# Sparse attention with a mixture layer on one core: K of two batches kept on chip for the first sparse pairs

## The chip, the cores and the metric

One core of one Trainium2 chip runs the whole program. The time is microseconds on the device, the median of several runs; lower is better. The engines of the core are TensorE (PE, with PEld for its weight loads), VectorE (DVE), ScalarE (ACT), GpSimd (POOL) and SyncE (SP); DMA transfers are issued from the queues of SP, ACT and POOL.

## The reference

Block-sparse attention over 4 batches, 8 heads, 768 positions and head dimension 64, followed by one feed-forward layer; all inputs are float32. A query block of 32 sees the first and last block, its neighbours, itself, and three sampled blocks (the first and last query block see everything):

```python
scores = scale * np.matmul(q, k.transpose(0, 1, 3, 2))
mask = np.abs(blk_i - blk_j) <= 1
mask = mask | (blk_i == 0) | (blk_j == 0) | (blk_i == n_blocks - 1) | (blk_j == n_blocks - 1)
for qb in range(n_blocks):
    for kb in sampled_blocks[qb]:
        mask[qb * 32:(qb + 1) * 32, kb * 32:(kb + 1) * 32] = True
attn = softmax(np.where(mask, scores, -1e9))      # then @ v
x = attn_out.transpose(0, 2, 1, 3).reshape(3072, 512)
h = x @ w_in                                      # 512 x 2048
g = h * (1.0 / (1.0 + np.exp(-1.702 * h)))
return g @ w_out                                  # 2048 x 512
```

The weights arrive as 64-bit floats and are taken apart on the chip.

## The kernel before

The 3072 rows of x are 48 units of 64 rows, and 8 units are a chunk of 512 rows. The first four units are the dense ones, one per batch: the first and the last query block against all 24 key blocks. Each has four items (two pairs of head pairs, two halves of the keys). The other 44 are sparse: a pair of query blocks u of two batches (0 and 1, or 2 and 3) shares one K entry and one V entry, and each batch is one unit and one item. A sparse K entry has 12 slots of 32 keys for two batches: slots 0 to 2 and 9 to 11 are the sampled blocks of the two query blocks, 3 to 5 and 8 their neighbourhood, 6 and 7 the first and the last block.

K, Q and V entries live in rings of two buffers (`RING`; `kg`, `qt`, `vown`, `vmid`). `loads` (L227) issues the load of an entry when, in the order of the program, the last use of the entry two before it has been issued. `load_k` (L180) loads Q of the entry and K: four transfers for a dense unit; for a sparse pair the neighbourhood (L195, L196), the first and last block where the buffer doesn't hold them yet (L198), and six sampled slots with an address from a register (L205), three of them from the POOL queue while `early` is set. `load_v` (L207) loads V; for sparse pairs the sampled and neighbouring rows come by two gathers on the POOL queue (L223), the rest by SP (L219, L221).

The program has two stages. `first` (L713), the opening, runs the items of the first nine units, 16 dense and 5 sparse ones (items 0 to 20), with `early` set. For each item n it issues the scores of n on PE (L284 dense, L272 sparse), the running minimum on DVE (L295), the transposes of item n-1 (L323, copied out on ACT at L327), the exponentials of n on ACT (L302), what ACT has to do for the weights (the list `late`), the values of n-1 (L356 dense, L348 sparse), and then `loads`. Between them `weights` (L425) is stepped, at fixed items: it fetches the 64-bit words of a weight tile (`raw`, L447, three buffers, asked for two tiles ahead, from the ACT queue), turns them into float32 (`a`, three buffers; L456 on ACT, L490, L496, L500 on DVE), splits the result in two float32r parts (L503 on ACT, L464 on DVE), and for the second weight saves it (`ws`, L471) for later chunks. Each engine executes in the order in which the program issues to it.

Then come 96 ticks of `tick` (L673): six chunks of 16 tiles f of the inner dimension, each with the up product (L538 to L540), the gate and the down product (L585 to L590); the items of the next chunk are laid between them by `plan`. In the first 16 ticks the remaining weight tiles are converted; `win` keeps the 16 tiles of w_in, 4 KB per partition each.

Of the kernel before, what the change touches and what calls it, by code (L numbers as in the profile page):

```python
# [9 lines left out]
F32 = mybir.dt.float32  # L10
F32R = mybir.dt.float32r
# [7 lines left out]
P = 128  # L19
# [14 lines left out]
NN = CT // P  # L34
RING = 2
WRING = 3
LAG = 1
QT = 4
BIG = float(2 ** 33)
# [4 lines left out]
class Kernel:  # L44
# [4 lines left out]
    def __init__(self, ctx, tc, q, qd, kb, kT, v, vd, sb, w_in, w_out, out):  # L49
        self.tc, self.nc = tc, tc.nc  # L50
        self.q, self.qd, self.kb, self.kT, self.v, self.vd, self.sb = q, qd, kb, kT, v, vd, sb
        self.w64, self.out = (w_in.bitcast(I32), w_out.bitcast(I32)), out
        pool = lambda name, bufs, **k: ctx.enter_context(tc.tile_pool(name=name, bufs=bufs, **k))
        self.const = pool("const", 1)
        self.work = pool("work", 2)
        self.small = pool("small", 6)
        psum = pool("psum", 1, space=PSUM)
        dram = pool("dram", 1, space=DRAM)
        self.ws = [dram.tile([P, DM], F32, name=f"ws{f}") for f in range(NF)]
        self.bank = [psum.tile([P, 512], F32, name=f"bank{i}") for i in range(8)]  # L60
        c = self.const


        self.kg = [c.tile([P, 12, 2, NPAIR * BLK], F32, name=f"kg{i}") for i in range(RING)]
        self.qt = [c.tile([P, 2, NPAIR * UT], F32, name=f"qt{i}") for i in range(RING)]
        self.vown = [c.tile([P, 2, 2 * DM], F32, name=f"vown{i}") for i in range(RING)]
        self.vmid = [c.tile([P, 2 * DM], F32, name=f"vmid{i}") for i in range(RING)]
        self.win = [c.tile([P, 2 * DM], F32R, name=f"win{f}") for f in range(NF)]
        self.wout = [c.tile([P, 2 * DM], F32R, name=f"wout{i}") for i in range(WRING)]
        self.x = [(c.tile([P, NCT, CT], F32R, name=f"xhi{i}"), c.tile([P, NCT, CT], F32R, name=f"xlo{i}"))  # L70
                  for i in range(2)]
        self.kmidof, self.vmidof = [None] * RING, [None] * RING
        self.units, self.kent, self.vent, self.items = [], [], [], []

        def entry(of, **more):
            of.append({"n": len(of), "scores": 0, "values": 0, **more})
            return of[-1]

        def item(k, v, **more):
            k["scores"] += 1  # L80
            v["values"] += 1
            self.items.append({"n": len(self.items), "unit": self.units[-1], "k": k, "v": v, **more})

        for b in range(B):
            entry(self.units, b=b, u=None)
            k = entry(self.kent, b=b, u=None)
            for i in range(2):
                v = entry(self.vent, b=b, u=None, i=i)
                for half in range(2):
                    item(k, v, i=i, half=half, first=i + half == 0, end=i + half == 2)  # L90
        for b0 in range(0, B, 2):
            for u in range(NU):
                k, v = (entry(of, b=b0, u=u) for of in (self.kent, self.vent))
                for b in (b0, b0 + 1):
                    entry(self.units, b=b, u=u)
                    item(k, v, first=True, end=True)
        self.knext = self.vnext = 0
        self.early = True


# [76 lines left out]

    def load_k(self, e):  # L180
        nc, b, u = self.nc, e["b"], e["u"]
        r = e["n"] % RING
        kg = self.kg[r].rearrange("p n b c -> p n (b c)")
        if u is None:
            nc.sync.dma_start(out=self.qt[r][:, 0], in_=self.qd[:, b])
            kg, kT = (ap.rearrange("p (a s) -> p a s", a=NPAIR) for ap in (self.kg[r].rearrange("p n b c -> p (n b c)"), self.kT[b]))
            for i in range(2):
                for half in range(2):
                    at = slice(2 * i, 2 * i + 2), slice(S // 2 * half, S // 2 * (half + 1))
                    nc.sync.dma_start(out=kg[:, at[0], at[1]], in_=kT[:, at[0], at[1]])  # L190
            self.kmidof[r] = None
            return
        q0, kb = 2 * u + 1, self.kb[:, b // 2]
        nc.sync.dma_start(out=self.qt[r].rearrange("p b c -> p (b c)"), in_=self.q[:, b // 2, u])
        nc.sync.dma_start(out=kg[:, 3:6].rearrange("p n c -> p (n c)"), in_=kb[:, q0 - 1:q0 + 2].rearrange("p n c -> p (n c)"))  # L195
        nc.sync.dma_start(out=kg[:, 8], in_=kb[:, q0 + 2])  # L196
        if self.kmidof[r] != b:
            nc.sync.dma_start(out=kg[:, 6:8], in_=kb[:, 0:NB:NB - 1])  # L198
            self.kmidof[r] = b
        for j in range(2):  # L200

            queue = nc.gpsimd if self.early and j == 1 else nc.sync
            for i in range(NR):
                at = queue.value_load(self.sbr[0:1, q0 + j, i, 0:1], min_val=0, max_val=NB - 1)
                queue.dma_start(out=kg[:, 9 * j + i], in_=kb[:, bass.ds(at, 1)].rearrange("p o c -> p (o c)"))  # L205

    def load_v(self, e):  # L207
        nc, b, u = self.nc, e["b"], e["u"]
# [17 lines left out]

    def loads(self):  # L227

        more = True
        if not self.knext:  # L230
            self.load_k(self.kent[0])
            for e in self.vent[:RING]:
                self.load_v(e)
            self.knext, self.vnext = 1, RING
        while more:
            more = False
            if self.knext < len(self.kent) and (self.knext < RING or not self.kent[self.knext - RING]["scores"]):
                self.load_k(self.kent[self.knext])
                self.knext += 1
                more = True  # L240
            if self.vnext < len(self.vent) and (self.vnext < RING or not self.vent[self.vnext - RING]["values"]):
                self.load_v(self.vent[self.vnext])
                self.vnext += 1
                more = True
# [11 lines left out]
    def scores(self, g):  # L256
# [7 lines left out]
        if sparse:  # L264
            bi, n = un["b"] % 2, 2 * P
            kg = self.kg[r][:, :, bi].rearrange("p n (a s) -> p n a s", a=NPAIR)
            for i in range(2):
                for a in range(2):
                    for j in range(2):
                        for h in range(2):  # L270
                            pair, rows, c = 2 * i + a, slice(D * h, D * (h + 1)), 2 * a + j
                            nc.tensor.matmul(  # L272
                                sps[h][BLK * c:BLK * (c + 1), n * i:n * (i + 1)].rearrange("p (n s) -> p n s", s=BLK),
                                self.qt[r][rows, bi, UT * pair + BLK * j:UT * pair + BLK * (j + 1)],
                                kg[rows, 4 * j:4 * j + 8, pair], start=True, stop=True, tile_position=(D * h, BLK * c))
            parts = [(i, 0) for i in range(2)]
            bias = self.bias[:, un["u"]].rearrange("p (n o) -> p n o", o=1).broadcast_to([P, 8, BLK])
        else:
            kt = self.kg[r].rearrange("p n b c -> p (n b c)").rearrange("p (a s) -> p a s", a=NPAIR)
            i, half, n = g["i"], g["half"], S // 2  # L280
            for a in range(2):
                for h in range(2):
                    pair, rows = 2 * i + a, slice(D * h, D * (h + 1))
                    nc.tensor.matmul(sps[h][UT * a:UT * (a + 1), 0:n], self.qt[r][rows, 0, UT * pair:UT * (pair + 1)],  # L284
                                     kt[rows, pair, n * half:n * (half + 1)], start=True, stop=True, tile_position=(D * h, UT * a))
            parts = [(i, half)]
            bias = self.zero.broadcast_to([P, n])
# [137 lines left out]
    def weights(self):  # L425
# [11 lines left out]
        def scalar(f):  # L437
            if self.early:
                self.late.append(f)
            else:  # L440
                f()

        def fetch(k):
            def go():
                f, i = todo[k]
                raw = self.work.tile([P, 2 * DM], I32, name="raw", bufs=3)
                nc.scalar.dma_start(out=raw, in_=self.w64[i][f])  # L447
                tiles[k] = {"raw": raw.rearrange("p (a b) -> p a b", b=2)}

            if k < len(todo):  # L450
                scalar(go)

        def first(k):
            def go():
# [29 lines left out]
        for k, (f, i) in enumerate(todo):  # L484
# [2 lines left out]
            fetch(k + 2)  # L487
            raw, a = tiles[k]["raw"], tiles[k]["a"]
            low, high = raw[:, :, 0], raw[:, :, 1]
            nc.vector.tensor_scalar(out=a, in0=a, scalar1=3, scalar2=None, op0=ALU.logical_shift_left)  # L490
            yield
            rested = not self.early
# [320 lines left out]
```

## Time and profile before

| | |
|---|---|
| time, median of 3 runs | 773.05 us (771.04 to 773.26) |
| profiled execution, time | 774.74 us |
| profiled execution, span | 773.1 us |
| PE busy | 734.6 us (95%) |
| DVE busy | 412.9 us (53%) |
| ACT busy | 385.0 us (50%) |
| POOL busy | 53.2 us (7%) |
| bytes moved by DMA | 128.22 MB, 166 GB/s over the span |

The busy shares are means over the whole span; the stages differ, so the rows further down are taken stage by stage. Times in a trace count from the first instruction of the span. A row of the timeline gives start, length, engine, source line, operation, output and input, and in brackets how long the engine stood idle before it and what ended that.

### The profile page before, as it was taken

To read this page: it belongs to the slowest core of one execution; us is meant where nothing else is said; L and a number is where in the kernel's file an instruction comes from. 1 tells how busy PE (TensorE), PEld (TensorE's weight loads), DVE (VectorE), ACT (ScalarE), POOL (GpSimd) and SP (SyncE) were. 2 spreads that over 40 slices of the span, in tenths; PEclk is the share of its full clock that TensorE was granted. 3 is DMA by queue.
4 is the path that set the end of the run, shared out by engine and by line. 5 is a ranking of instruction groups with operands and counts; after the bars stand their busy time and mean duration, and the time that the engine had idled before them with its cause. 6 is when DMAs were issued, how large, how long until landed. Compare 5 with 4: busy or idle time off the path is not lost.

```text
span 773.1 us, 19315 instructions
## 1 busy us (share of the span) xinstructions
PE 734.6 (95%) x7584; PEld 571.4 (74%) x7584; DVE 412.9 (53%) x1076; ACT 385.0 (50%) x950; POOL 53.2 (7%) x79
## 2 busy tenths in 40 slices
PE   4986599999999999999999999999999999999997
PEld 2554477777777877877877877877877877888885
DVE  2885478998854454454454454454464454343333
ACT  3885466766645445445445445445444444333232
POOL 1022210110100000000000000000000000000000
PEclk9999899999999999999999999999999999999999
DMA  8999888788656435566444455434465410141111
GB/s 292 336 340 318 263 259 273 241 249 288 204 144 190 133 119 166 155 167 189 138 121 146 146 171 164 131 123 155 133 164 173 129 43 29 42 110 41 55 42 54
DMA packets 65469, 128.22 MB, mean 166 GB/s; under 512 B 7761, under 2 KB 31570, under 8 KB 65378
## 3 DMA queue, kind: packets, MB, share of 16 engines
q1 hardware_dynamic: 51202, 80.76, 34.6%
q0 software_dynamic: 6944, 24.72, 10.2%
q10 hardware_dynamic: 7232, 21.50, 8.4%
q8 instruction: 60, 0.98, 0.5%
q14 instruction: 31, 0.25, 0.1%
HBM read 116.47 MB, written 10.49 MB: 164 GB/s over the span
## 4 chain that ended last, share of the span: by engine, by line
PE 77%; DMA 9%; DVE 6%; ACT 4%; issue 2%; SPq 1%; ACTq 0%; DVEq 0%
PE bank L538 11%; PE bank L540 10%; PE bank L590 10%; PE bank L589 10%; PE bank L585 10%; PE bank L539 10%; PE bank L272 5%; PE bank L348 5%; PE bank L323 4%; DMA kg<-in_kb_dram 3%; DMA vown<-in_vd_dram 2%; DMA raw<-in_moe_w_in_dram 1%; ACT ex L302 1%; PE bank L356 1%; PE bank L411 1%
## 5 line engine op out<-in xcount | busy, mean ns | idle before, releaser
L538 PE MATMUL bank<-xhi,win 128*128 128x512 f32 x384 | 158.3, 412 | 1.6 <-DVE g L553 1.2
L553 DVE SCALAR_TENSOR_TENSOR g<-g,bank 128x512 f32<-128x512 f32 x83 | 57.1, 688 | 186.9 <-ACT g L546 186.9
L590 PE MATMUL bank<-wout,ghi 128*128 128x512 f32 x384 | 152.0, 396 | 0.0
L589 PE MATMUL bank<-wout,ghi 128*128 128x512 f32 x384 | 151.9, 396 | 0.0
L540 PE MATMUL bank<-xhi,win 128*128 128x512 f32 x384 | 151.1, 393 | 0.0
L539 PE MATMUL bank<-xlo,win 128*128 128x512 f32 x384 | 149.9, 390 | 0.0
L302 ACT ACTIVATE ex<-bank,nm 128x256 f32<-128x256 f32 (+1 forms) x208 | 99.8, 492 | 98.5 <-DVE nm L295 98.3
L546 ACT ACTIVATE g<-bank 128x512 f32<-128x512 f32 x96 | 57.6, 600 | 148.6 <-PE bank L540 148.6
L585 PE MATMUL bank<-wout,glo 128*128 128x512 f32 x384 | 107.7, 394 | 0.0
L527 DVE TENSOR_TENSOR wout<-wst,wout 128x512 fp32r<-128x512 f32 x80 | 55.5, 693 | 91.5 <-ACT wout L526 91.2
L558 ACT CAST ghi<-g 128x512 fp32r<-128x512 f32 x96 | 59.6, 620 | 70.8 <-DVE g L553 70.8
L538 PEld LDWEIGHTS bank<-xhi,win 128*128 128x128 f32 x384 | 72.1, 188 | 19.5 <-ACT wst L551 1.8
L585 PEld LDWEIGHTS bank<-wout,glo 128*128 128x128 f32 x384 | 72.5, 189 | 17.3
L590 PEld LDWEIGHTS bank<-wout,ghi 128*128 128x128 f32 x384 | 72.5, 189 | 16.8
L589 PEld LDWEIGHTS bank<-wout,ghi 128*128 128x128 f32 x384 | 72.1, 188 | 16.6
L540 PEld LDWEIGHTS bank<-xhi,win 128*128 128x128 f32 x384 | 72.1, 188 | 16.3
L327 ACT COPY pt<-bank 128x512 f32<-128x512 f32 (+1 forms) x120 | 61.3, 561 | 42.9 <-PE bank L323 42.4
L295 DVE CUSTOM_DVE_ANT_1 bank<-bank,bias 128x256 f32<-128x256 f32 x176 | 73.9, 440 | 15.2 <-PE bank L272 12.2
L539 PEld LDWEIGHTS bank<-xlo,win 128*128 128x128 f32 x384 | 72.3, 188 | 13.0
L223 POOL DMA_INDIRECT vown<-in_v_dram,vidx x44 | 43.2, 982 | 512.8 <-PE bank L348 490.9
L323 PEld LDWEIGHTS bank<-ident,ex 128*128 128x128 f32 x448 | 52.3, 144 | 21.5 <-ACT ex L302 9.0
L566 DVE TENSOR_TENSOR glo<-g,ghi 128x512 fp32r<-128x512 f32 x96 | 65.7, 685 | 0.7 <-ACT ghi L558 0.7
(75 smaller groups left out, 788.8 us busy)
## 6 DMA issues: line engine op xcount, KB each, us to landing
wst<-ws SPq DMA_DIRECT2D x80, 256.0 KB, 2.8
kg<-in_kb_dram SPq DMA_DIRECT2D x142, 128.0 KB, 3.0
kg<-in_kb_dram SPq DMA_DIRECT2D x22, 384.0 KB, 5.4
raw<-in_moe_w_in_dram ACTq DMA_DIRECT2D x16, 512.0 KB, 6.7
raw<-in_moe_w_out_dram ACTq DMA_DIRECT2D x16, 512.0 KB, 4.4
kg<-in_kT_dram SPq DMA_DIRECT2D x16, 384.0 KB
vown<-in_vd_dram SPq DMA_DIRECT2D x8, 768.0 KB, 5.9
qt<-in_q_dram SPq DMA_DIRECT2D x22, 256.0 KB
```

The costliest lines, as they stand in the source:

```text
L295: nc.vector.tensor_tensor_reduce(out=at, in0=at, in1=bias, scale=-SCALE, scalar=3.0e38, op0=ALU.add, op1=ALU.min, accum_out=un["nm"][:, ha ...
L302: nc.scalar.activation(out=ex, in_=sps[h][:, n * k:n * (k + 1)], func=AF.Exp, bias=un["nm"][:, half, c:c + 1], scale=-1.0, accum_out=un["r ...
L323: nc.tensor.transpose(ps[:, m], g["ex"][h, i][:, k * P:(k + 1) * P], self.ident)
L327: copies.append(lambda pt=pt, ps=ps, m=m: nc.scalar.copy(out=pt[:, 0:m], in_=ps[:, 0:m]))
L538: nc.tensor.matmul(h, wih[:, k], hi[:, k], start=(k == 0), stop=False)
L539: nc.tensor.matmul(h, wih[:, k], lo[:, k], start=False, stop=False)
L540: nc.tensor.matmul(h, wil[:, k], hi[:, k], start=False, stop=(k == NCT - 1))
L558: self.nc.scalar.copy(out=ghi, in_=self.g[m][0])
L566: self.nc.vector.tensor_tensor(out=glo, in0=g, in1=ghi.bitcast(F32), op=ALU.subtract)
L585: nc.tensor.matmul(o[n], glo[:, tk[n]], woh, start=False, stop=last)
L589: nc.tensor.matmul(o[n], ghi[:, tk[n]], woh, start=(f == 0), stop=False)
L590: nc.tensor.matmul(o[n], ghi[:, tk[n]], wol, start=False, stop=False)
```

## The change

The dense units are taken in the order of batches 2, 3, 0, 1. K of the dense units of batches 0 and 1 goes into a buffer of its own, `kres`, instead of the ring. While `early` is set, K of a sparse pair is copied from `kres` to the slots of `kg` by GpSimd, one copy per slot (128 partitions x 256 float32), 12 or 10 per pair; for the six sampled slots the block's number is loaded into a register first. These copies are issued to GpSimd's queue where `loads` reaches the entry: entries 4 and 5 need not wait for the two dense entries before them, which no longer use the ring. The load of Q is a step of its own. A fourth buffer for weight words, `raw4`, is used by every fourth tile while `early` is set, and words are asked for three tiles ahead there. `kres` and `raw4` take the place of the tiles 9 to 15 of `win` (28 KB per partition), which are allocated when the conversion comes to tile 9.

```diff
+NWIN = 9
-        self.win = [c.tile([P, 2 * DM], F32R, name=f"win{f}") for f in range(NF)]
+        self.win = [c.tile([P, 2 * DM], F32R, name=f"win{f}") for f in range(NWIN)]
...
+        self.opening = ExitStack()
+        early = self.opening.enter_context(tc.tile_pool(name="opening", bufs=1))
+        self.kres = early.tile([P, 2, NPAIR, S], F32, name="kres")
+        self.raw4 = early.tile([P, 2 * DM], I32, name="raw4")
...
-        for b in range(B):
+        for b in (2, 3, 0, 1):
             entry(self.units, b=b, u=None)
...
+    def load_q(self, e):
+        b, u, qt = e["b"], e["u"], self.qt[e["n"] % RING]
+        if u is None:
+            self.nc.sync.dma_start(out=qt[:, 0], in_=self.qd[:, b])
+        else:
+            self.nc.sync.dma_start(out=qt.rearrange("p b c -> p (b c)"), in_=self.q[:, b // 2, u])
...
         if u is None:
-            nc.sync.dma_start(out=self.qt[r][:, 0], in_=self.qd[:, b])
+            k = e["kt"] = self.kres[:, b] if b < 2 else self.kg[r].rearrange("p n b c -> p n (b c)").rearrange("p (a s) -> p a s", a=NPAIR)
...
-                    nc.sync.dma_start(out=kg[:, at[0], at[1]], in_=kT[:, at[0], at[1]])
-            self.kmidof[r] = None
+                    nc.sync.dma_start(out=k[:, at[0], at[1]], in_=kT[:, at[0], at[1]])
+            if b >= 2:
+                self.kmidof[r] = None
             return
-        q0, kb = 2 * u + 1, self.kb[:, b // 2]
-        nc.sync.dma_start(out=self.qt[r].rearrange("p b c -> p (b c)"), in_=self.q[:, b // 2, u])
+        q0, middle = 2 * u + 1, self.kmidof[r] != b
+        self.kmidof[r] = b
+        if self.early:
+            kg = self.kg[r].rearrange("p n b (a s) -> p n b a s", s=BLK)
+            src = self.kres.rearrange("p b a (n s) -> p n b a s", s=BLK)
+            for n, at in [(3, q0 - 1), (4, q0), (5, q0 + 1), (8, q0 + 2)] + [(6, 0), (7, NB - 1)] * middle:
+                nc.gpsimd.tensor_copy(out=kg[:, n], in_=src[:, at])
+            for j in range(2):
+                for i in range(NR):
+                    at = nc.gpsimd.value_load(self.sbr[0:1, q0 + j, i, 0:1], min_val=0, max_val=NB - 1)
+                    nc.gpsimd.tensor_copy(out=kg[:, 9 * j + i], in_=src[:, bass.ds(at, 1)].rearrange("p o b a s -> p (o b) a s"))
+            return
...
-            queue = nc.gpsimd if self.early and j == 1 else nc.sync
...
     def loads(self):
+        k = self.kent
+        passed = lambda n: n < RING or not k[n - RING]["scores"]
+
+        def kfree(n):
+            e = k[n]
+            last = e["n"] - (4 if e["u"] is not None and e["n"] < 6 else RING)
+            return n < RING or not k[last]["scores"]
...
+            if self.qnext < len(k) and passed(self.qnext):
+                self.load_q(k[self.qnext])
+                self.qnext += 1
+                more = True
+            if self.knext < self.qnext + self.early and self.knext < len(k) and kfree(self.knext):
+                self.load_k(k[self.knext])
...
+        asked = [0]
+
         def fetch(k):
-            def go():
+            def go(k, own):
                 f, i = todo[k]
-                raw = self.work.tile([P, 2 * DM], I32, name="raw", bufs=3)
+                raw = self.raw4 if own else self.work.tile([P, 2 * DM], I32, name="raw", bufs=3)
...
+            for n in range(asked[0], min(k + 1 + self.early, len(todo))):
+                scalar(lambda n=n, own=self.early and n % 4 == 3: go(n, own))
+                asked[0] += 1
...
+            if i == 0 and f == NWIN:
+                self.opening.close()
+                late = self.pool("late", 1)
+                self.win += [late.tile([P, 2 * DM], F32R, name=f"win{n}") for n in range(NWIN, NF)]
```

## Rows read from the trace of the kernel before

**Rows 1.** Busy time by stretch: from:to, length, each engine busy, granted PE clock, DMA share, GB/s.
```profile
8.00:58.00 50.00, 43.36 (x581) 27.47 (x583) 38.78 (x144) 37.56 (x110) 4.88 (x7) 1.00 0.99 352
58.00:98.50 40.50, 25.21 (x604) 17.54 (x599) 20.90 (x79) 19.49 (x63) 10.49 (x14) 0.87 0.93 288
98.50:215.00 116.50, 113.31 (x1127) 87.67 (x1124) 98.37 (x228) 79.61 (x184) 8.34 (x8) 1.00 0.77 247
```
**Rows 2.** Timeline of PE, end of the dense part and sparse items 16 to 19.
```profile
57.38 0.92 PE L356 MATMUL bank<-vown,pt 128*64 128x64 f32 x24 [1.18 <-DMA vown<-in_vd_dram]
58.23 1.09 PE L272 MATMUL bank<-kg,qt 64*32 64x256 f32 x32
...
65.01 1.37 PE L356 MATMUL bank<-vown,pt 128*64 128x64 f32 x24 [4.89 <-ACT pt L327]
66.31 1.96 PE L272 MATMUL bank<-kg,qt 64*32 64x256 f32 x32
...
69.80 0.30 PE L348 MATMUL bank<-vown,pt 128*32 128x64 f32 x2
...
72.61 1.32 PE L272 MATMUL bank<-kg,qt 64*32 64x256 f32 x32 [1.45 <-DMA vmid<-in_v_dram]
...
78.02 1.09 PE L272 MATMUL bank<-kg,qt 64*32 64x256 f32 x32
```
**Rows 3.** Timeline of PE, the last sparse item and the first up matmul.
```profile
89.06 2.34 PE L272 MATMUL bank<-kg,qt 64*32 64x256 f32 x32 [7.26 <-DMA kg<-in_kb_dram]
...
98.48 0.50 PE L538 MATMUL bank<-xhi,win 128*128 128x512 f32 x1
```
**Rows 4.** Timeline of ACT and its queue, 54 to 64 us.
```profile
54.53 0.34 ACTq L471 DMA_DIRECT2D ws<-a  x1
...
63.93 0.66 ACT L456 ACTIVATE a<-raw 128x512 f32<-128x512 f32 x1 [5.88 <-DMA ws<-a]
```
**Rows 5.** Timeline of SP's queue, the last dense V load.
```profile
49.89 0.38 SPq L212 DMA_DIRECT2D vown<-in_vd_dram  x1
```
**Rows 6.** Transfers of the first 100 us, total.
```profile
DMA packets 13834, 30.80 MB, mean 308 GB/s; under 512 B 1486, under 2 KB 8655, under 8 KB 13819
```
**Rows 7.** Transfers of 42 to 58 us: total, and the sparse K loads issued.
```profile
DMA packets 2089, 5.24 MB, mean 328 GB/s; under 512 B 277, under 2 KB 1054, under 8 KB 2087
...
kg<-in_kb_dram SPq DMA_DIRECT2D x2, 384.0 KB, 11.8
kg<-in_kb_dram SPq DMA_DIRECT2D x5, 128.0 KB, 4.3
...
kg<-in_kb_dram POOLq DMA_DIRECT2D x4, 128.0 KB, 5.6
kg<-in_kb_dram SPq DMA_DIRECT2D x1, 256.0 KB
```
**Rows 8.** Transfers of the first 40 us, the ring of SP.
```profile
q1 hardware_dynamic: 5393, 10.39, 72.8%
```
**Rows 9.** Groups by line on POOL: busy us, mean ns of one.
```profile
masks.py:199 POOL TENSOR_SCALAR_AFFINE_SELECT ident<-ident 128x128 f32<-128x128 f32 x1 | 0.3, 294 | 0.1
masks.py:197 POOL MEMSET ident<- 128x128 f32 x1 | 0.2, 220 | 0.0
L142 POOL MEMSET zero<- 128x1 f32 x1 | 0.1, 104 | 0.1
```
**Rows 10.** Timeline of POOL: gathers of V of pair 0, a K transfer.
```profile
54.49 1.48 POOL L223 DMA_INDIRECT vown<-in_v_dram,vidx  x1 [9.23 <-DVE a L500]
56.28 0.98 POOL L223 DMA_INDIRECT vown<-in_v_dram,vidx  x1 [0.30 <-PE bank L323]
...
69.86 0.57 POOL L205 DMA_DIRECT2D kg<-in_kb_dram  x1 [0.60 <-issue]
```
**Rows 11.** Line L223 in 40 to 100 us, from issue to landing.
```profile
DMA to landing us min/median/max: 5.8/9.3/10.6
```
**Rows 12.** Busy time of VectorE in 42 to 58 us, line L496 alone.
```profile
42.00:58.00 16.00, 1.84 (x3) 1.00 0.99 328
```

More of the change, by code (lines that the diff above doesn't have):

```diff
@@ L52, in __init__ @@
         self.w64, self.out = (w_in.bitcast(I32), w_out.bitcast(I32)), out
-        pool = lambda name, bufs, **k: ctx.enter_context(tc.tile_pool(name=name, bufs=bufs, **k))
+        self.ctx = ctx
+        pool = self.pool = lambda name, bufs, **k: ctx.enter_context(tc.tile_pool(name=name, bufs=bufs, **k))
         self.const = pool("const", 1)
@@ L96, in __init__ @@
                     item(k, v, first=True, end=True)
-        self.knext = self.vnext = 0
+        self.qnext = self.knext = self.vnext = 0
         self.early = True
@@ L182, in load_k @@
         r = e["n"] % RING
-        kg = self.kg[r].rearrange("p n b c -> p n (b c)")
         if u is None:
-            nc.sync.dma_start(out=self.qt[r][:, 0], in_=self.qd[:, b])
-            kg, kT = (ap.rearrange("p (a s) -> p a s", a=NPAIR) for ap in (self.kg[r].rearrange("p n b c -> p (n b c)"), self.kT[b]))
+            k = e["kt"] = self.kres[:, b] if b < 2 else self.kg[r].rearrange("p n b c -> p (n b c)").rearrange("p (a s) -> p a s", a=NPAIR)
+            kT = self.kT[b].rearrange("p (a s) -> p a s", a=NPAIR)
             for i in range(2):
@@ L189, in load_k @@
                     at = slice(2 * i, 2 * i + 2), slice(S // 2 * half, S // 2 * (half + 1))
-                    nc.sync.dma_start(out=kg[:, at[0], at[1]], in_=kT[:, at[0], at[1]])
-            self.kmidof[r] = None
+                    nc.sync.dma_start(out=k[:, at[0], at[1]], in_=kT[:, at[0], at[1]])
+            if b >= 2:
+                self.kmidof[r] = None
             return
-        q0, kb = 2 * u + 1, self.kb[:, b // 2]
-        nc.sync.dma_start(out=self.qt[r].rearrange("p b c -> p (b c)"), in_=self.q[:, b // 2, u])
+        q0, middle = 2 * u + 1, self.kmidof[r] != b
[10 more added lines that the diff above has]
+            return
+        kg, kb = self.kg[r].rearrange("p n b c -> p n (b c)"), self.kb[:, b // 2]
         nc.sync.dma_start(out=kg[:, 3:6].rearrange("p n c -> p (n c)"), in_=kb[:, q0 - 1:q0 + 2].rearrange("p n c -> p (n c)"))
         nc.sync.dma_start(out=kg[:, 8], in_=kb[:, q0 + 2])
-        if self.kmidof[r] != b:
+        if middle:
             nc.sync.dma_start(out=kg[:, 6:8], in_=kb[:, 0:NB:NB - 1])
-            self.kmidof[r] = b
         for j in range(2):
-            queue = nc.gpsimd if self.early and j == 1 else nc.sync
             for i in range(NR):
-                at = queue.value_load(self.sbr[0:1, q0 + j, i, 0:1], min_val=0, max_val=NB - 1)
-                queue.dma_start(out=kg[:, 9 * j + i], in_=kb[:, bass.ds(at, 1)].rearrange("p o c -> p (o c)"))
+                at = nc.sync.value_load(self.sbr[0:1, q0 + j, i, 0:1], min_val=0, max_val=NB - 1)
+                nc.sync.dma_start(out=kg[:, 9 * j + i], in_=kb[:, bass.ds(at, 1)].rearrange("p o c -> p (o c)"))
     def load_v(self, e):
@@ L227, in loads @@
     def loads(self):
-        more = True
[L230 to L234, printed above, removed]
+        k = self.kent
[4 more added lines that the diff above has]
+            return n < RING or not k[last]["scores"]
+        more = True
         while more:
             more = False
-            if self.knext < len(self.kent) and (self.knext < RING or not self.kent[self.knext - RING]["scores"]):
-                self.load_k(self.kent[self.knext])
+            if self.qnext < len(k) and passed(self.qnext):
[4 more added lines that the diff above has]
+                self.load_k(k[self.knext])
                 self.knext += 1
                 more = True
-            if self.vnext < len(self.vent) and (self.vnext < RING or not self.vent[self.vnext - RING]["values"]):
+            while self.vnext < len(self.vent) and (self.vnext < RING or not self.vent[self.vnext - RING]["values"]):
                 self.load_v(self.vent[self.vnext])
@@ L278, in scores @@
         else:
-            kt = self.kg[r].rearrange("p n b c -> p (n b c)").rearrange("p (a s) -> p a s", a=NPAIR)
+            kt = g["k"]["kt"]
             i, half, n = g["i"], g["half"], S // 2
@@ L441, in scalar @@
                 f()
+        asked = [0]
         def fetch(k):
-            def go():
+            def go(k, own):
                 f, i = todo[k]
-                raw = self.work.tile([P, 2 * DM], I32, name="raw", bufs=3)
+                raw = self.raw4 if own else self.work.tile([P, 2 * DM], I32, name="raw", bufs=3)
                 nc.scalar.dma_start(out=raw, in_=self.w64[i][f])
                 tiles[k] = {"raw": raw.rearrange("p (a b) -> p a b", b=2)}
-            if k < len(todo):
-                scalar(go)
+            for n in range(asked[0], min(k + 1 + self.early, len(todo))):
+                scalar(lambda n=n, own=self.early and n % 4 == 3: go(n, own))
+                asked[0] += 1
         def first(k):
```

## The prediction

> **What bounds the kernel now.** I read the stages first (busy time by stretch), then PE in order of time at the seams that they show, then what ended each wait, then the transfers, last GpSimd, whose load the change raises. Of the span, 98.5 us are the opening (attention of the first nine units, before the first up matmul, L538); from there PE is busy 113.3 of 116.5 us [rows 1], so what the opening saves moves the rest forward, and what it doesn't save can hardly be won later. In the opening PE is busy 43.4 of 50 us in the dense part and 25.2 of 40.5 us in the sparse part, while the DMA engines are at 0.99 and 0.93 of their time [rows 1]: the transfers set the pace, in the sparse part above all. The reader is to see the holes of PE there [rows 2, 3]: 1.18 us before 57.38 (V of the last dense unit), 4.89 before 65.01, 1.45 before 72.61 (vmid) and 7.26 before 89.06 (K of pair 2). The second is put down to ScalarE, but ScalarE itself stood 5.88 us for the save of a weight word that it had asked for at 54.53 [rows 4]: the transfer queue again.
>
> **What the change takes from the queue.** A K entry of a sparse pair is 12 slots of 128 KB the first time a ring buffer is used for it and 10 after (slot size: [rows 7]). By the code `first()` still has `early` set when it loads entry 7 (after item 19), so four pairs, not three, are copied by GpSimd: 12+12+10+10 slots, 5,632 KB = 5.77 MB of the 30.80 MB of the first 100 us [rows 6]. The fourth word buffer asks for one 512 KB word earlier: +0.52 MB. At the 308 GB/s of that stretch the balance is 17.0 us of queue time. That is a ceiling, since compute lies beside it; the sum goes along PE's chain.
>
> **The chain, term by term** (s16 to s20 are the score groups of the five sparse items, at 58.23, 66.31, 72.61, 78.02 and 89.06; the first L538 is at 98.48 [rows 2, 3]).
>
> 1. Dense end. The V load of the last dense unit left SP at 49.89 [rows 5], behind all SP transfers of pair 0's K; now only Q stands there. I take the 1.18 us as gone: s16 at 57.05. Ends: 0 and 1.18. The dense stretch before it has no sparse K in front of it and is left as it is; the new batch order issues the same 16 dense K transfers.
>
> 2. The save of the word. In 42 to 58 us the queue moved 5.24 MB; the sparse K loads issued there are 2 x 384 + 5 x 128 + 256 KB on SP and 4 x 128 KB on GpSimd's queue, 2.23 MB or 43% [rows 7]. The save took from 54.53 to 63.9, 9.4 us; at 57% of it, 5.4, it lands at 59.9, against 58.05 (63.93 - 5.88) when ScalarE came to wait [rows 4]. ScalarE then waits 1.9 and PE, which saw 1 us less, about 1: 4.0 us go (ends 0 and 4.89). The earlier word fetch covers the read of a word, not this reuse of its result buffer, so I give it nothing of its own. s17: 66.31 - 1.18 - 4.0 = 61.1; the value products of item 16, 3.49 us behind s17 (69.80 [rows 2]), could start at 64.6.
>
> 3. The vmid wait, 1.45 us: by the code SP issued pair 1's six K transfers ahead of vmid; it goes (ends 0 and 1.45). s18 could be at 61.1 + 6.30 - 1.45 = 66.0.
>
> 4. GpSimd, the cost. It executes in order: copies of pair 0 (asked for after s7), of pair 1 (after s11), two gathers of V of pair 0 (after the values of item 13, which ended at 54.5, when they left [rows 10]), two of pair 1, copies of pair 2, and so on. Copies of pair 0 wait for K of batch 1, the last dense K; no one on PE waited for that transfer. SP's ring had moved 10.39 MB by 40 us [rows 8]; the bytes up to and with that K are 4 x 128 + 16 x 384 + 5 x 768 KB = 10.75 MB, 1.1 us more at 328 GB/s [rows 7], and the extra word 1.6: 42.7.
> One copy is 128 x 256 f32. No row shows one. MEMSET takes 104 ns for 1 column and 220 for 128, so 0.34 us for 256 by its slope; the affine select, which also reads, takes 294 for 128, so 0.49 by its [rows 9]; the far end is a gather, 0.98 [rows 10]. I take 0.42, between the element rows. A register load before each of six sampled slots shows as 0.60 us between two GpSimd DMAs (69.86 [rows 10]); beside a running copy some of it hides, and I take 0.5 of 0.26 to 0.6. A pair of 12 copies costs C = 12 x 0.42 + 6 x 0.5 = 8.0 us; ends 12 x 0.34 + 6 x 0.26 = 5.6 and 12 x 0.49 + 6 x 0.6 = 9.5, far end 12 x 0.98 + 3.6 = 15.4. Pair 0 is done at 50.7, before s16; pair 1 at 58.7. The gathers of V of pair 0, which left at 54.49 and 56.28 [rows 10], then leave at 58.7 and 60.5. Landing took 5.8 to 10.6, median 9.3 us, in the full queue [rows 11]; I take 6.5 in the lighter one: 67.0 against 64.6. So a new wait of 2.4 us opens before the values of item 16. s18: 68.4.
>
> 5. s18 to s19 was 5.41 us; I keep it. s19 to s20 was 11.04 with the 7.26 for K, which goes; the 3.8 that stay were read with VectorE and ScalarE already drained, so I take 5.41 again (ends 3.8 and 5.41): s20 at 79.2. Pair 2's ten copies start after s17 and the gathers of pair 1 (66) and end near 73, in time. Late next is V of pair 2: issued at 73 to 76, landed by 83, needed about 1 us before the first L538.
>
> 6. s20 to the first L538 was 9.42 us with PE partly at the lower of its two levels, 1.2 against 2.4 GHz (granted 0.87 over the sparse part [rows 1]): s20 took 2.34 us against 1.09 for s16 [rows 2, 3], behind a hole of 7 us. Without the hole I take 8.2. First L538 at 87.4, 11.1 us earlier.
>
> Behind it nothing changes in order or count: the weight steps go by items, so as many words are ready, and K of later pairs is loaded as before. The span of 773.1 becomes 762.0; the profiled execution took 774.74, 1.69 above the median of the runs, so by the median 773.05 - 11.1 = **762.0**. Without the GpSimd wait, without the rest in term 2 and with 4.2 us twice in term 5 the gain is 16.9 (756); with C = 9.5 and 8 us of landing it is 6.6.
>
> A rule speaks against it. The row first: in 42 to 58 us VectorE ran 7 operations with two operands in SBUF (L496 three times, L500 and L464 twice each, 0.6 us apiece or a little more), 4.6 us, 29% of the time [rows 12], and no GpSimd operation that reads SBUF lay beside one. The Trainium skill, SBUF — State Buffer, section "SBUF: two separate sides", says that VectorE and GpSimd share one pair of ports that is locked for a whole instruction, also between a VectorE operation with two SBUF inputs and a GpSimd one that reads SBUF. No run here shows it yet; rival a) is what it would do.
>
> **The rivals.** As long as V of pair 0 comes last, the first L538 is at 71.4 + 2C (42.7 + 2C + 1.8 issue + 6.5 landing, 1.4 to s18, 2 x 5.41, 8.2).
> a) Copies and VectorE's two-operand operations exclude each other. A copy then waits on average 0.29 x 0.3 = 0.1 us, C = 9.2, and 7 operations on VectorE wait up to 0.42 each. VectorE is busy 38.8 of 50 us in the dense part [rows 1], so most of that is absorbed; at most 2.9 isn't: L538 at 89.8 to 92.7, gain 5.8 to 8.7, 766.
> b) The queue stays full. 30.80 - 5.77 + 0.52 = 25.6 MB; 17.6 of it moves by 58 at 352 GB/s, the other 8.0 at 288 end at 86 [rows 1], no earlier than the forecast. Then transfers land as late as now: the save costs its 4.9 again, the gathers take 9.3 and set the later end, 42.7 + 16 + 1.8 + 9.3 = 69.8 for the values of item 16: L538 at 90.2, gain 8.3, 765. Against it: V of pair 3 and a word are in these bytes and not needed by then.
> c) No change: the copies replace the transfers. C = 12.5 to 14.5 gives 96.4 to 100.4, about 2 us to either side: 771 to 775.
> d) Slower: GpSimd becomes the bound of the opening. Place: its queue, K copies in front of V gathers. Above C = 13.5 (0.82 us a copy with the register loads unhidden) the change loses; at 1.0 us, C = 15.6, L538 is at 102.6 and the time 777. For it: a GpSimd DMA with a register address comes every 1.17 us [rows 10]; against: its element rows are a third of that [rows 9].
> e) It does less than it says: K of batches 0 and 1 still comes only at its old place in the ring, and if V or a word in front of it is late, so are pairs 0 and 1; each microsecond of that is one of s18. That belongs to the spread of a) and b), not to another sign.
>
> **How the numbers follow.** Forecast (gain 8.5 to 14) 0.47, better (14 to 18) 0.10, a) and b) 0.22, c) 0.08, d) 0.13. A change of 0.3% (2.3 us, about what a measurement can tell here) separates the signs: faster 0.47 + 0.10 + 0.22 = 0.79, same 0.08, slower 0.13. The range runs from 756, most of the better case, to 770.5, where a) and b) end with the spread of C up to 12; c) and d) lie outside.
>
> **What would show it.** Right: no sparse K transfer issued before the first L538; DMA share in 58 to 85 us below 0.93; no hole of 7 us before s20; ScalarE's wait for the save under 2 us; GpSimd busy with copies of 0.3 to 0.5 us from about 43; a hole of 1 to 4 us before the values of item 16, ended by V; first L538 at 82 to 92 and the rest of the span as long as now. Wrong: copies near 0.8 us or more, V of pair 0 or 1 late by more than 6 us, VectorE operations of twice their length beside copies, or a stage behind the first L538 that grows by what the opening saved.

## The result and the profile after

The changed kernel takes 764.84 us (762.95 to 766.15, 4 runs) against 773.03 us: ratio 0.9898 (0.9869 to 0.9927). Two later measurements, each beside the kernel before on one chip, gave 763.27 us, 0.9892 (0.9861 to 0.9923), and 764.94 us, 0.9895 (0.9860 to 0.9930). So it is about 1.05% faster; the forecast was 762.0 us.

Busy time by stretch, columns as in [rows 1]; the third stretch has the length of the third of before and starts at the first up matmul, L573 here:
```profile
8.00:58.00 50.00, 42.42 (x616) 26.84 (x616) 40.58 (x144) 37.73 (x111) 12.41 (x26) 1.00 0.95 340
58.00:98.50 40.50, 34.44 (x718) 24.21 (x703) 30.84 (x101) 28.48 (x83) 13.65 (x26) 0.96 0.75 240
...
86.60:203.10 116.50, 112.15 (x1118) 86.59 (x1119) 97.88 (x228) 78.68 (x182) 8.75 (x8) 1.00 0.76 243
```
The dense part takes as long as it did (49.2 us from the first scores to the first sparse ones, against 49.5); inside it the DMA share rose to 1.04 in 8 to 40 us (before 0.99) and fell to 0.68 in 40 to 50 (before 0.98), where K of the first pair had moved. The sparse part has PE at 34.4 us of 40.5 against 25.2, at a DMA share of 0.75 against 0.93. The stage behind is unchanged within about 1 us: from the first L573 to the end it is 762.2 - 86.5 = 675.7 us, before 773.1 - 98.5 = 674.6, in two other profiles of the changed kernel 673.9 and 674.2. All of the gain is in the opening. The transfers up to the first up matmul, before (98.48 us) and changed (86.52 us):
```profile
DMA packets 13709, 30.35 MB, mean 308 GB/s; under 512 B 1468, under 2 KB 8637, under 8 KB 13695
```
```profile
DMA packets 9865, 25.13 MB, mean 290 GB/s; under 512 B 946, under 2 KB 5555, under 8 KB 9852
```

The timeline of PE at the same places as [rows 2, 3] (L300 are the sparse scores, L376 and L384 the values, L439 a transpose):
```profile
32.52 0.92 PE L384 MATMUL bank<-vown,pt 128*64 128x64 f32 x24 [2.06 <-DMA vown<-in_vd_dram]
...
50.31 0.44 PE L439 MATMUL bank<-ident,x 128*128 128x128 f32 x2 [0.99 <-DVE x L432]
...
57.25 1.09 PE L300 MATMUL bank<-kg,qt 64*32 64x256 f32 x32
...
60.32 1.09 PE L300 MATMUL bank<-kg,qt 64*32 64x256 f32 x32
...
66.11 0.24 PE L376 MATMUL bank<-vown,pt 128*32 128x64 f32 x1 [1.56 <-DMA vown<-in_v_dram,vidx]
...
67.53 1.96 PE L300 MATMUL bank<-kg,qt 64*32 64x256 f32 x32
...
72.28 1.09 PE L300 MATMUL bank<-kg,qt 64*32 64x256 f32 x32
...
76.35 0.30 PE L376 MATMUL bank<-vown,pt 128*32 128x64 f32 x2 [1.74 <-ACT pt L355]
...
77.65 1.09 PE L300 MATMUL bank<-kg,qt 64*32 64x256 f32 x32
...
86.52 0.50 PE L573 MATMUL bank<-xhi,win 128*128 128x512 f32 x1
```
The holes of [rows 2, 3], of 1.18, 4.89, 1.45 and 7.26 us, are all gone. New are 2.06 us for V of a dense unit, 0.99 for VectorE, 1.56 for V of pair 0, which was not late before, and 1.74 that the profile puts down to ScalarE, before the values of item 18; what held ScalarE there is open.

ScalarE at the place of [rows 4] (L502 saves a word, L487 reads the next into the buffer of an older one):
```profile
54.31 0.34 ACTq L502 DMA_DIRECT2D ws<-a  x1
...
57.80 0.69 ACT L487 ACTIVATE a<-raw 128x512 f32<-128x512 f32 x1
```
It stood 5.88 us there before and stands for nothing now: the save landed within 3.5 us of 54.31.

GpSimd, 36 to 60 us (L212 the fixed slots, L216 the sampled ones, L244 the gathers of V; before: [rows 10]):
```profile
39.58 2.90 POOL L212 COPY kg<-kres 128x256 f32<-128x256 f32 x6 [34.64 <-DMA kres<-in_kT_dram]
42.43 2.38 POOL L216 COPY kg<-kres 128x256 f32 x5
45.49 0.71 POOL L216 COPY kg<-kres 128x256 f32 x1 [0.69 <-issue]
46.15 2.11 POOL L212 COPY kg<-kres 128x256 f32<-128x256 f32 x6
48.21 2.30 POOL L216 COPY kg<-kres 128x256 f32 x6
54.37 1.40 POOL L244 DMA_INDIRECT vown<-in_v_dram,vidx  x1 [3.86 <-DVE a L535]
56.08 0.95 POOL L244 DMA_INDIRECT vown<-in_v_dram,vidx  x1 [0.30 <-PE bank L351]
```
All 24 copies of two pairs fit into 10.9 us; GpSimd then stood 3.9 us for VectorE, and the gathers left at the time they did before.

### The profile page after: what moved, and what is told of

It is laid out like the page before. It is cut to its first block, busy times and chain, and to the rows that moved or that the text cites. A ratio compares the mean times of both kernels' runs of the same rounds, so it can differ in the third digit from the quotient of the medians.

```text
span 762.2 us, 19295 instructions
## 1 busy us (share of the span) xinstructions
PE 731.1 (96%) x7584; PEld 568.3 (75%) x7584; DVE 415.3 (54%) x1076; ACT 384.9 (51%) x950; POOL 64.2 (8%) x111
## 4 chain that ended last, share of the span: by engine, by line
PE 79%; DMA 7%; DVE 6%; ACT 4%; issue 2%; ACTq 0%; SPq 0%; DVEq 0%
PE bank L573 11%; PE bank L575 10%; PE bank L625 10%; PE bank L624 10%; PE bank L620 10%; PE bank L574 10%; PE bank L376 5%; PE bank L300 5%; PE bank L351 4%; DMA ws<-a 2%; DMA vown<-in_vd_dram 2%; DMA raw<-in_moe_w_out_dram 2%; DMA vown<-in_v_dram,vidx 1%; PE bank L439 1%; DVE bank L323 1%
## 5 line engine op out<-in xcount | busy, mean ns | idle before, releaser
L573 PE MATMUL bank<-xhi,win 128*128 128x512 f32 x384 | 158.3, 412 | 2.0 <-DVE g L588 1.6
L573 PEld LDWEIGHTS bank<-xhi,win 128*128 128x128 f32 x384 | 72.1, 188 | 19.7 <-DVE g L588 2.0
L244 POOL DMA_INDIRECT vown<-in_v_dram,vidx x44 | 43.0, 977 | 494.3 <-PE bank L376 480.5
L574 PEld LDWEIGHTS bank<-xlo,win 128*128 128x128 f32 x384 | 72.3, 188 | 13.0
```

What stands on the lines that cost most here:

```text
L573: nc.tensor.matmul(h, wih[:, k], hi[:, k], start=(k == 0), stop=False)
L574: nc.tensor.matmul(h, wih[:, k], lo[:, k], start=False, stop=False)
```

## The experiments

The theory was that the gain is the 5.77 MB of K that leave a full queue; the rivals, that it is the order (Q and V no longer behind K on SP) or the fourth word buffer. Ratios are against the kernel before, measured beside it.

**K by transfers again, all else as changed.**
```diff
-        if self.early:            # copies by GpSimd
+        if False:
...
-                at = nc.sync.value_load(...)
+                at = queue.value_load(...)     # queue: GpSimd's for j == 1 while early
```


> The changed kernel, but the first four sparse pairs get K by transfers again (three of six sampled slots from GpSimd's queue, as before); K of batches 0 and 1 still lies in its own buffer, Q is still loaded apart and earlier, the fourth word buffer stays. Theory (the gain is K's bytes off the full queue): 5.77 MB return, first L538 at 95 to 99, 771 to 775 us, and a hole for K before one of the sparse score groups returns. Rival 1 (the gain is the order: Q and V no longer wait behind K on SP) and rival 2 (it is the fourth word buffer): both are still in, so 764 to 767 us.


771.90 us, 0.9975 (0.9959 to 0.9991); first up matmul at 98.6. The timeline of PE:
```profile
51.03 1.55 PE L385 MATMUL bank<-vown,pt 128*64 128x64 f32 x24 [5.83 <-DMA vown<-in_vd_dram]
65.61 1.09 PE L301 MATMUL bank<-kg,qt 64*32 64x256 f32 x32
...
76.41 0.31 PE L377 MATMUL bank<-vown,pt 128*32 128x64 f32 x1 [4.57 <-DMA vown<-in_v_dram,vidx]
```
Its transfers up to the first up matmul, then the load of a dense V on SP's queue, changed and in this kernel:
```profile
DMA packets 13855, 30.98 MB, mean 314 GB/s; under 512 B 1477, under 2 KB 8623, under 8 KB 13841
```
```profile
36.33 6.05 SPq L233 DMA_DIRECT2D vown<-in_vd_dram  x2
```
```profile
43.99 1.82 SPq L234 DMA_DIRECT2D vown<-in_vd_dram  x2
```
The theory holds in size: most of the gain goes, 1.5 us of about 9 stay. (The profiled execution, 775.44 us, was the slowest of 12.) It missed the place. K was asked for earlier than in the kernel before, so it was not K that came late but V, dense and sparse. What is left of the change here (Q ahead, K asked for earlier, the word buffer) is worth 0.25%. One thing is not parted: the dense V stands behind six K transfers on SP's queue again and leaves 7.7 us later than in the changed kernel, and no run has K's bytes without K's place ahead of V. Two things speak for the bytes. In the profiles of the three kernels that transfer K for the first pairs, 30.4 to 31.1 MB move up to the first up matmul and it comes at 98.1 to 98.6 us; in all others it is 24.5 to 25.3 MB and 82.7 to 89.6 us (93.2 with the doubled copies below). And this kernel comes out near the kernel before, although it asks for Q and K earlier.

**Three word buffers; the fourth alone.**
```diff
 # three word buffers, on the changed kernel
-            for n in range(asked[0], min(k + 1 + self.early, len(todo))):
+            for n in range(asked[0], min(k + 1, len(todo))):
```
```diff
 # the fourth alone, on the kernel before: fetch and raw4 as in the change, nothing else
+            for n in range(asked[0], min(k + 1 + self.early, len(todo))):
+                scalar(lambda n=n, own=self.early and n % 4 == 3: go(n, own))
```


> The changed kernel with three word buffers, asked for two tiles ahead, as before. Theory: no loss, 763 to 766 us; the wait of 2.1 us for V of a dense unit near 32 us, which the earlier word brought, shrinks below 1 us, first L538 at 85 to 88. Rival 2 (the fourth buffer carries the gain): ScalarE stands for a word again by 4 us or more, 768 to 773 us.

> The kernel before with the fourth word buffer alone. Theory: 772 to 775 us, first L538 at 97 to 101, the hole of some 7 us before the last sparse score group stays. Rival 2: 765 to 769 us, ScalarE's wait of 5.9 us gone.


Three buffers: 763.46 us, 0.9854 (0.9830 to 0.9877). The fourth alone: 773.58 us, 0.9994 (0.9967 to 1.0020), first up matmul at 98.1. PE with the fourth alone, then with three:
```profile
64.82 1.47 PE L361 MATMUL bank<-vown,pt 128*64 128x64 f32 x24 [4.35 <-ACT pt L332]
...
76.01 2.27 PE L277 MATMUL bank<-kg,qt 64*32 64x256 f32 x32 [5.05 <-DMA kg<-in_kb_dram]
```
```profile
44.88 0.92 PE L383 MATMUL bank<-vown,pt 128*64 128x64 f32 x24 [1.35 <-DMA vown<-in_vd_dram]
...
69.21 0.32 PE L375 MATMUL bank<-vown,pt 128*32 128x64 f32 x1 [5.05 <-DMA vown<-in_v_dram,vidx]
```
The fourth word buffer gives nothing by itself, and without it ScalarE doesn't stand for a word. With the fourth alone the hole for K did not stay before the last sparse scores, where it was expected; it is 5.05 us and before the scores of item 18. The 2.06 us hole near 32 us is not there with three; a smaller one is at 44.9, and V of pair 0 is late by 5 us in this profile, so its first up matmul (87.7) is no earlier. Measured again, beside the changed kernel:


> The changed kernel with three word buffers, once more, beside it on one chip: 762 to 764.5 us. If the earlier word costs by filling the queue in the first 40 us, 0.5 to 2 us below the changed kernel; if the word buffer does nothing at all, within 0.5 us.

> The changed kernel as it is, for the comparison of this call: 763 to 765.5 us.


763.77 us, 0.9866 (0.9825 to 0.9908), against 764.94 for the changed kernel: 1.2 us lower, but the intervals overlap. That the earlier word costs time is likely, not shown.

**Copies twice.**
```diff
                 nc.gpsimd.tensor_copy(out=kg[:, n], in_=src[:, at])
+                nc.gpsimd.tensor_copy(out=kg[:, n], in_=src[:, at])
```
and the same at the sampled slots.


> The changed kernel with every GpSimd copy of K issued twice, the second onto the first. In the changed kernel the 24 copies of pairs 0 and 1 took from 39.6 to 50.5 us. If GpSimd's queue is the next bound (rival d of the prediction, short of its point), the doubled copies end near 61 to 63, the gathers of V of pair 0 leave 7 to 9 us later than now and land at 72 to 75 instead of 66, first L538 at 92 to 96: 770 to 774 us. If GpSimd has slack (4 us stood idle before the gathers), only part of that appears: 764 to 767 us.

> The changed kernel as it is, to stand beside the others of this call on the same chip: 763 to 766 us, first L538 at 86 to 90.


770.56 us, 0.9971 (0.9953 to 0.9990), with the changed kernel at 763.27 beside it. GpSimd, then PE:
```profile
67.88 1.03 POOL L246 DMA_INDIRECT vown<-in_v_dram,vidx  x1 [0.46 <-issue]
69.21 0.95 POOL L246 DMA_INDIRECT vown<-in_v_dram,vidx  x1 [0.30 <-issue]
```
```profile
72.30 0.39 PE L378 MATMUL bank<-vown,pt 128*32 128x64 f32 x2 [9.45 <-DMA vown<-in_v_dram,vidx]
...
74.30 0.31 PE L378 MATMUL bank<-vown,pt 128*32 128x64 f32 x1 [1.41 <-DMA vown<-in_v_dram,vidx]
```
GpSimd is the next bound, and three quarters of the gain (7.3 of 9.8 us) are lost at twice the copies: the slack is 3.9 us. The gathers left 13 us late, later than expected, since a doubled pair took 15.1 us (the first) and 12.7. In a queue that had been empty (DMA share 0.00 in 64.0 to 67.8 us) they landed within 4.4 and 5.1 us (67.88 to 72.30, 69.21 to 74.30), where the changed kernel's second took 10.0 (56.08 to 66.11, at a share of 0.94). Its own instruction took 0.95 us on GpSimd in both, and in the changed kernel it left no later than before the change, so the copies are not what makes V late there. That it is the queue fits, but VectorE, too, was idle in 67.8 to 72.3 us of the doubled kernel and busy for 9.4 of the 11.7 us from 54.4 in the changed one; no run parts the two.

**Fills in place of copies.** These kernels leave K of the four pairs out: each copy is a fill with zeros, which writes the same slot but reads nothing. Without a source the fills ran 20 us before the copies' time, so a second kernel lets them wait for K with two copies of one column.
```diff
-                nc.gpsimd.tensor_copy(out=kg[:, n], in_=src[:, at])
+                nc.gpsimd.memset(kg[:, n], 0.0)
 # second kernel, ahead of each pair's fills:
+            for b in range(2):
+                nc.gpsimd.tensor_copy(out=kg[:, 3, b, 3, 0:1], in_=self.kres[:, b, 3, S - 1:S])
```


> The changed kernel with each GpSimd copy of K replaced by a fill of the same slot with zeros, so the four pairs see no K (the output differs there); the register loads stay. Copies and fills write alike, but a fill reads no SBUF. If VectorE's operations beside the copies were longer (0.74 against 0.43 us for one of 128 x 256 with two SBUF operands) because both read SBUF, they are back to 0.43 and 0.69, the 1 us hole of PE near 50 us goes, 762 to 764.5 us. Rival (any GpSimd instruction lengthens them): they stay long, as the changed kernel, 764 to 766 us.

> As the fills before, but ahead of each pair's fills two copies of one column from K of batches 0 and 1, so that the fills run at the time of the copies, beside VectorE's work from 39 us on (K is left out again and the output differs). If it is reading SBUF by both that lengthens VectorE's operations, they stay at 0.42 to 0.43 us (128 x 256, two SBUF operands), 0.68 (128 x 512) and 0.17 (4 and 8 columns) beside the fills; time 761.5 to 764. Rival (any GpSimd work, or writing): 0.5 to 0.9 and 0.3 as beside the copies; 763 to 766.


762.96 us, 0.9886 (0.9854 to 0.9919), and 763.90 us, 0.9876 (0.9840 to 0.9911), 1.0 below the changed kernel beside it. VectorE's groups in 39.5 to 50.6 us (busy us, mean ns), first before, then changed:
```profile
L464 DVE TENSOR_TENSOR win<-a,win 128x512 fp32r<-128x512 f32 x2 | 1.4, 684 | 0.0
...
L404 DVE TENSOR_TENSOR x<-x,pt 128x256 f32<-128x256 f32 x1 | 0.4, 426 | 0.0
...
L390 DVE TENSOR_TENSOR ri<-f,rg 128x8 f32<-128x8 f32 x1 | 0.2, 167 | 0.0
...
L384 DVE TENSOR_TENSOR rf<-rs,f 128x8 f32<-128x8 f32 x1 | 0.2, 161 | 0.0
```
```profile
L495 DVE TENSOR_TENSOR win<-a,win 128x512 fp32r<-128x512 f32 x2 | 1.6, 782 | 0.0
...
L432 DVE TENSOR_TENSOR x<-x,pt 128x256 f32<-128x256 f32 x1 | 0.7, 736 | 0.0
...
L418 DVE TENSOR_TENSOR ri<-f,rg 128x8 f32<-128x8 f32 x1 | 0.4, 432 | 0.0
...
L412 DVE TENSOR_TENSOR rf<-rs,f 128x8 f32<-128x8 f32 x1 | 0.4, 391 | 0.0
```
Now the fills beside VectorE (second kernel), GpSimd and then VectorE in order of time:
```profile
46.56 0.82 POOL L218 MEMSET kg<- 128x256 f32 x3
...
48.28 0.31 POOL L218 MEMSET kg<- 128x256 f32 x1 [0.29 <-issue]
48.89 0.31 POOL L218 MEMSET kg<- 128x256 f32 x1 [0.29 <-issue]
```
```profile
46.41 0.68 DVE L497 TENSOR_TENSOR win<-a,win 128x512 fp32r<-128x512 f32 x1
...
48.21 0.17 DVE L414 TENSOR_TENSOR rf<-rs,f 128x8 f32<-128x8 f32 x1
...
49.02 0.17 DVE L420 TENSOR_TENSOR ri<-f,rg 128x8 f32<-128x8 f32 x1
```
Two of the three operations on 8 columns take 0.39 and 0.43 us beside copies (the third stays at 0.17), and all take 0.17 beside fills: the added 0.2 to 0.3 us are less than one copy. So it is GpSimd's reading of SBUF that holds VectorE up, and not GpSimd's work as such or its writing; and VectorE's operations with their source in PSUM take as long beside copies as before (0.42 us for one of 128 x 256). What it costs the kernel is at most the 1 us hole near 50 us; in the times it can't be told from nothing.

**A buffer of its own for V of pair 0.**
```diff
+        self.vx = (early.tile([P, 2, 2 * DM], F32, name="vownx"), early.tile([P, 2 * DM], F32, name="vmidx"))
...
+            last = {8: 0, 10: 6}.get(n, n - RING)     # the V entry that must be done before entry n loads
```


> The changed kernel with a buffer of its own for V of the first sparse pair (12 KB more per partition in the opening, tiles 6 to 15 of the up weight allocated late): its gathers are asked for after item 12 instead of 14, and those of pair 2 two items earlier. If the V landing at 66.1 us is what ends the hole before the values of item 16, the gathers leave near 50.5, land near 60, the 1.6 us hole and most of the lower clock behind it go: first L538 at 83.5 to 85, 762 to 763.5 us. Rival (the queue only carries a fixed sum, or VectorE paces this stretch): V lands in time, but the same time is lost at the next wait, 764 to 766 us.


765.07 us, 0.9872 (0.9848 to 0.9895): a gain is not shown. The interval overlaps that of the changed kernel, which was not measured beside it, and three word buffers gave 0.9854 there. PE, then ScalarE, in its slowest execution (766.24), the one profiled:
```profile
63.92 1.55 PE L392 MATMUL bank<-vown,pt 128*64 128x64 f32 x24 [3.00 <-ACT pt L363]
```
```profile
62.84 0.66 ACT L495 ACTIVATE a<-raw 128x512 f32<-128x512 f32 x1 [3.13 <-DMA ws<-a]
```
V is in time, and the save of the word is late, as in the rival; that V's earlier gathers are what delays it is likely, not shown. So the next kernel takes both buffers and drops the fourth word buffer.
```diff
+        self.a4 = early.tile([P, DM], I32, name="a4")
-                a = tiles[k]["a"] = self.work.tile([P, DM], I32, name="a", bufs=3)
+                a = tiles[k]["a"] = self.a4 if own else self.work.tile([P, DM], I32, name="a", bufs=3)
```


> The changed kernel without the fourth word buffer, with the own buffer for V of the first sparse pair and with a fourth buffer for the float32 result of a weight tile (2 KB) in the opening, so that ScalarE need not stand for the save of a word. If the waits behind 58 us are two single transfers in the way (V's gather, then the save: with the V buffer alone PE stood 3.0 us for ScalarE, which stood 3.1 for the save), both go: first L538 at 82 to 85, 759 to 762 us. Rival (the queue carries a fixed sum and the wait moves to the next transfer): 763 to 766 us, with a third wait for a DMA in 58 to 80 us.

> The kernel with own buffers for V of the first pair and for a fourth result tile and without the fourth word buffer, once more, beside the changed kernel on one chip. If its two waits were single ones, 759.5 to 762.5 us and 1 to 3 us below the changed kernel; if the earlier 1.7 us were chance, the two are within 0.8 us.


761.53 us, 0.9868 (0.9837 to 0.9900), and 762.83, 0.9874 (0.9837 to 0.9910): 1.7 and 2.1 us below the changed kernel beside it, though the intervals against the kernel before overlap. It has the lowest median of the kernels measured together, both times. PE in the two runs:
```profile
69.36 0.24 PE L384 MATMUL bank<-vmidx,pt 128*32 128x64 f32 x1 [2.29 <-issue]
...
82.71 0.50 PE L581 MATMUL bank<-xhi,win 128*128 128x512 f32 x1
```
```profile
67.02 0.32 PE L384 MATMUL bank<-vownx,pt 128*32 128x64 f32 x1 [3.40 <-ACT pt L363]
...
86.27 0.50 PE L581 MATMUL bank<-xhi,win 128*128 128x512 f32 x1
```
Neither wait for a DMA is left behind 58 us. The first up matmul came at 82.7 in the first run, whose profiled execution (758.98 us) was the fastest of its six, but at 86.3 in the second (763.01 us): no earlier than in the changed kernel, and later than the 82 to 85 expected of the first run; the second time is 0.3 us above its range. What is left are 2.3 and 3.4 us at the values of the first sparse pair, for which the profile names no cause (in the second run PE stood for ScalarE, which itself had stood 4.7 us for what the profile calls remote); what it is stays open.

## Why the prediction came out right, and where it did not

- **Bound and size.** The transfers were the bound of the opening, K's transfers are most of the gain, and the stage behind moved by about 1 us. By the profiles the gain is 773.1 - 762.2 = 10.9 us against 11.1; by medians 8.2, 9.8 and 8.7 in three measurements. Of the 2.7 us between 10.9 and 8.2, 1.7 are my base: I subtracted a sum made on the profiled execution, 1.7 us above its median, from the median. The other 0.9 is that the profiled execution after lies that far below its own median. How much of the 1.7 lay in the opening is not shown: in three profiles of the changed kernel the first up matmul is at 86.5, 87.9 and 88.9, while the rest of the span differs by up to 1.8 us.
- **Term 1** (57.05; measured 57.25): the wait on the last dense V went. The sum is right by chance. The first scores start 0.7 us earlier; the first two items take 7.9 us to the second value group and not 9.5 (the same score group took 1.56 us at 15.25 before and 0.88 at 13.91 now, with 1.00 granted in both; the reason is open); waits of 1.10 and 1.18 on dense V go. Against that stand the two new holes (2.06 and 0.99) and 0.6 us of smaller ones. I had called the dense stretch unchanged.
- **Terms 2 and 3** (s17 61.1; measured 60.32): the save's wait went whole, not but for 1 us, since the save landed within 3.5 us and not in 5.4; vmid's went.
- **Term 4** failed in its cause. One copy takes 0.44 to 0.46 us on the mean, against the 0.42 that I took. But the register loads cost next to nothing behind running copies (24 copies at 0.46 are 11.1 us, and all of it took 10.9, with one gap of 0.69 inside): a pair took (50.5 - 39.6) / 2 = 5.5 us, my lower end, not 8.0, and K of batch 1 was there at 39.6, not 42.7. GpSimd was done 8 us earlier than forecast and delayed no gather. The wait for V that I laid to it came all the same, 1.56 us (4.3 and 3.2 in the other two profiles) against 2.4, because the gather took 10.0 us to land and not 6.5: where it runs, the DMA engines are still at 0.94 and 0.89 of their time (50 to 60, 60 to 70 us). That looks like rival b) inside the forecast, with VectorE's part open, as said above. Behind that hole PE ran at a granted clock of 0.83 over 60 to 70 us: s18 took 1.96 us, not 1.09.
- **Terms 5 and 6** (10.8 and 8.2; measured 72.28 - 67.53 + 77.65 - 72.28 = 10.1 and 8.9): sizes only.
- **Rival a)** is real: the Trainium skill, SBUF — State Buffer, section "SBUF: two separate sides", has such a lock between the two engines, and the traces agree that an operation of VectorE is held up (0.43 against 0.17 us). My sign of being wrong, operations of twice their length, came for these small ones, but its price on PE in the dense part is the 0.99 us hole at most, and not 2.9: the copies of two pairs lie beside VectorE for 10.9 us only, and VectorE absorbs most of what they add.
- **Rival b)** for the whole opening did not come: the DMA share in 58 to 85 us was 0.75. Its end at 86 also left out the 1.12 MB that had moved by 8 us; with them the remaining bytes end at 82.
- **Rivals c) and e)** did not come: a pair took 5.5 us, not the 12.5 that c) needs, and K of batch 1 was there 3 us earlier than I took, not later.
- **Rival d)** did not come, but has the right place: doubling the copies takes back 7.3 of 9.8 us (770.56 against 763.27), and even then the change does not lose.

## What to carry to other kernels

In a stretch where the DMA engines are full, count bytes: here 5.8 MB less were worth about 9 us, and the transfer that a wait names need not be the one that fills the queue. Moving K earlier in the full queue made V late; taking K off the queue gave the time back. Make the sum on the median execution, or say how far the profiled one lies from it in the stretch that the change touches.

## What the runs showed of the hardware that was not expected

A GpSimd copy of 128 x 256 f32 takes 0.40 us while VectorE is idle (the doubled copies behind 72.65 us), and a register load ahead of it shows mostly as 0.2 to 0.3 us or as nothing, against 0.60 between two GpSimd DMAs; once per profile of the changed kernel a gap of 0.47 to 0.69 us stands there (before 45.49 above), and why is open. A gather of 512 KB landed in 4.4 to 5.1 us in an empty queue beside an idle VectorE, and in 10.0 in a busy one beside a busy VectorE. VectorE operations that read SBUF can be held up by a GpSimd copy even when they have 8 columns (0.39 and 0.43 us against 0.17), and were not by a fill.
